# Layer A of two joined attentions: values issued behind the next group's scores

## The chip, the cores and the metric

The kernel runs on one core of a Trainium2 chip. The metric is device time in microseconds of one execution; the median of three runs stands for the kernel.

## The reference

Two attention layers over a sequence of 2048 rows with 1024 features, 32 heads of 32, in fp32; their outputs are joined along the last axis.

```python
# layer A: each query sees 8 keys, at distances 0, 2, ..., 14
idx = pos[:, None] - (jnp.arange(8) * 2)[None, :]
logits = einsum("bhsd,bhswd->bhsw", q, k[idx]) * scale      # masked where idx < 0
o = einsum("bhsw,bhswd->bhsd", softmax(logits), v[idx])
# layer B: each query sees the 256 keys up to itself
scores = einsum("bhqd,bhkd->bhqk", q, k) * scale            # masked outside the band
o = einsum("bhqk,bhkd->bhqd", softmax(scores), v)
# both: qkv = x @ wqkv before, o @ wo after
```

## The kernel before

**Units and groups.** The host lays the inputs out anew; layer A's rows are parted into even and odd ones, so that its dilated window becomes a plain band of 8. Each layer is four chunks of 512 rows. A chunk is a *unit* (layer B is units 0 to 3, layer A units 4 to 7), and in a unit the 32 heads are eight *groups* of four. `hg = 8 * u + s` numbers the groups, 0 to 63; layer A's are 32 to 63, and where the text counts "the 12th scores" it counts from 1 within layer A. In layer A half of the units have a `halo`: the last 8 keys and the last block of values of the unit before.

**Projections.** The large products, called g here (each into a tile `g` in PSUM), take most of TensorE's time: queries and keys (line 586), values into `vbuf` (line 654; 512 columns wide for groups 0 to 3, 256 wide for groups 4 and 5 and for 6 and 7), the output product of layer B (line 714), and the output product of layer A (line 773), which runs at the end. Each fp32 product is built of three products of parts (`TERMS`); ScalarE and VectorE cut the parts (lines 218, 221, 224) from tiles that POOL loads (line 173).

**Layer A's attention.** A group's queries and keys come out of `g` by ScalarE (lines 482 and 487) into `nat`; eight DMAs on the queue of SP gather them by head (line 506). `window` then builds two pieces of work for TensorE. `scores` (line 923) is 64 products of 32x32 tiles. VectorE adds the mask (line 931), takes the softmax (lines 941 to 959, with ScalarE's exponential on line 947) and transposes (line 961); ScalarE copies the result in eight pieces into a band of zeros called `wide` (lines 970 and 973). `values` (line 984) is 16 products, 20 with a halo, of `vbuf` by `wide`, each 32 columns of weights. `finish` copies them out of PSUM on ScalarE (line 1032), and SP stores them to `od` in DRAM (line 1037).

**What sets the order.** Nothing is scheduled by the compiler: while the program is built, a planner keeps a clock for each engine (`Clock`) and writes the instructions down in the order of its own simulation. Four sequences compete for TensorE: `aux`, `twos` (the values, in order), `ones` (the scores, in order) and `gemm` (the projections, in order). At each step the planner asks the head of each sequence when it could start, takes the earliest, and of equal ones the first in the order just given. What the piece triggers on other engines is issued at the planned times, so the order on ScalarE, VectorE and SP follows from the order on TensorE. For the values the question is `values_ready`: the group's part of `vbuf` is there, the last copy into `wide` is done, and the one PSUM bank for `o` is free. `done["scores"]` is filled by `seat_free` as soon as the scores of a group are issued.

The order that comes out, in pieces: in layer A TensorE has 55 unbroken runs of projections, with scores and values between them; of the 32 groups, 9 have their values right behind the scores of the next group, and 23 have them between projections.

## Time and profile before

| | us |
|---|---|
| median of three runs | 1814.6 (1813.79 to 1816.29) |
| profiled execution | 1818.1 |
| its span, first to last instruction | 1816.4 |
| TensorE busy with matmuls | 1789.4 (99%) |
| VectorE busy | 1262.0 (69%) |
| ScalarE busy | 924.4 (51%) |
| granted TensorE clock, mean | 0.995 |

The profile shows one execution. PE is TensorE's matmuls, PEld its weight loads, which run beside them; DVE is VectorE, ACT ScalarE, POOL GpSimd, SP the engine that only issues DMAs. A row of the timeline merges neighbouring instructions of one line: start, length, engine, line, operation, tile written and tiles read, count, and in brackets the idle time ahead of them with what ended it. "issue" is time in which the engine waited for nothing that the profile shows. The matmuls of the scores and values are in plain fp32 and count twice in the trace: 64 are x128. Since matmuls are pipelined, the ends overlap; distances are taken from start to start.

### The profile page before, as it was taken

The page shows a single profiled execution, that of the slowest core. Times are in us where ns is not written, and L with a number is a line of the kernel's source. Part 1 is how long each engine was busy: PE and PEld are TensorE (multiplying, and loading weights), DVE is VectorE, ACT ScalarE, POOL GpSimd, SP SyncE. Part 2 cuts the span into 40 slices and gives each one's busy share as a digit, 9 for nine tenths or more (in the row PEclk, how much of TensorE's full clock was granted, in tenths as well). Part 3 has the DMA queues.
Part 4 walks back from the last instruction along what each step waited for, and adds up shares of the span by engine and source line. Part 5 has one row for each costly group of instructions (what it writes and reads, how often), then busy time and mean ns, then how long its engine had stood idle before and what let it go on. Part 6 is the DMA issues. An engine that isn't in the chain of part 4 may idle for free.

```text
span 1816.4 us, 38617 instructions
## 1 busy us (share of the span) xinstructions
PE 1789.4 (99%) x14730; PEld 1465.3 (81%) x14730; DVE 1262.0 (69%) x2790; ACT 924.4 (51%) x2301; POOL 410.1 (23%) x950
## 2 busy tenths in 40 slices
PE   9999999999999999999999999999999999999999
PEld 6787878888777788778887788888888887888887
DVE  6677876768867769777677566646755766557866
ACT  5556466555655565656555344423542544446342
POOL 2313323222242223333224300101010011002220
PEclk9999999999999999999999999999999999999999
DMA  7354664544646555454545343536753674348984
GB/s 239 114 142 136 183 168 139 167 139 137 183 139 177 146 144 170 134 166 128 160 110 164 106 150 119 164 123 213 249 173 113 221 250 137 120 144 297 311 265 145
DMA packets 129241, 303.61 MB, mean 167 GB/s; under 512 B 16160, under 2 KB 31520, under 8 KB 129056
## 3 DMA queue, kind: packets, MB, share of 16 engines
q0 software_dynamic: 45216, 164.65, 28.7%
q1 hardware_dynamic: 73472, 116.56, 22.8%
q10 hardware_dynamic: 10368, 19.93, 3.0%
q8 instruction: 117, 1.92, 0.4%
q14 instruction: 68, 0.56, 0.1%
HBM read 189.79 MB, written 44.04 MB: 129 GB/s over the span
## 4 chain that ended last, share of the span: by engine, by line
PE 91%; DMA 3%; ACT 2%; DVE 2%; issue 1%; SPq 0%; POOL 0%; ACTq 0%; DVEq 0%; POOLq 0%
PE g L586 37%; PE g L654 18%; PE g L714 10%; PE g L773 8%; PE s L1172 5%; PE s L1089 5%; PE o L1219 5%; PE s L923 2%; PE o L984 2%; DMA r<-od 2%; DMA raw<-xs 1%; ACT wide L970 1%; ACT s L1099 0%; DVE w L224 0%; DVE r L846 0%
## 5 line engine op out<-in xcount | busy, mean ns | idle before, releaser
L586 PE MATMUL g<-x,w 128*128 128x512 f32 x3072 | 773.0, 396 | 2.8 <-ACT x L218 2.6
L586 PEld LDWEIGHTS g<-x,w 128*128 128x128 f32 x3072 | 568.1, 189 | 114.5 <-issue 6.8
L654 PE MATMUL g<-w,x 128*128 128x256 f32 (+1 forms) x2304 | 393.7, 322 | 0.5 <-issue 0.3
L224 DVE TENSOR_TENSOR w<-raw,w 128x512 fp32r<-128x512 f32 x518 | 339.4, 697 | 51.8 <-ACT w L218 45.1
L654 PEld LDWEIGHTS g<-w,x 128*128 128x128 f32 x2304 | 334.5, 192 | 28.8 <-issue 1.6
L1099 ACT ACTIVATE s<-s,nm 128x384 f32<-128x384 f32 (+2 forms) x512 | 274.4, 537 | 101.8 <-DVE nm L1094 101.6
L1094 DVE CUSTOM_DVE_ANT_0 s<-s,mask_d 128x384 f32<-128x384 f32 (+2 forms) x512 | 261.7, 554 | 88.1 <-PE s L1089 87.4
L1158 POOL TENSOR_SCALAR_AFFINE_SELECT pbuf<-pbuf 128x128 f32<-128x128 f32 (+1 forms) x606 | 220.1, 391 | 326.2 <-ACT pbuf L1179 324.8
L1179 ACT ACTIVATE pbuf<-s 128x384 f32<-128x384 f32 (+2 forms) x480 | 202.8, 505 | 73.7 <-PE s L1172 72.1
L714 PE MATMUL g<-r,w 128*128 128x512 f32 x768 | 190.8, 394 | 1.4 <-ACT r L1054 0.7
L173 POOL DMA_DIRECT2D raw<-wqk x126 | 68.6, 545 | 440.8 <-DVE w L224 303.0
L714 PEld LDWEIGHTS g<-r,w 128*128 128x128 f32 x768 | 141.9, 188 | 30.7 <-DVE r L1058 1.6
L773 PE MATMUL g<-x,w 128*128 128x512 f32 x672 | 153.2, 390 | 0.5 <-DVE w L224 0.5
L773 PEld LDWEIGHTS g<-x,w 128*128 128x128 f32 x672 | 126.0, 188 | 27.3 <-DVE w L224 0.9
L221 DVE CAST w<-raw 128x1024 fp32r<-128x1024 f32 x187 | 129.3, 692 | 25.2 <-PE g L586 22.6
L1172 PEld LDWEIGHTS s<-qst,kst 128*128 128x128 f32 x704 | 113.3, 189 | 40.6 <-ACT s L1099 16.2
L1089 PE MATMUL s<-kst,qst 96*128 96x384 f32 (+2 forms) x512 | 142.5, 342 | 0.9 <-ACT s L1099 0.7
L1172 PE MATMUL s<-qst,kst 128*128 128x256 f32 (+2 forms) x704 | 136.4, 302 | 3.5 <-ACT s L1099 3.0
L1089 PEld LDWEIGHTS s<-kst,qst 96*128 96x128 f32 x512 | 93.5, 189 | 25.8 <-issue 3.9
L931 DVE TENSOR_TENSOR band<-s,near 128x160 f32<-128x160 f32 x128 | 32.5, 316 | 116.0 <-PE s L923 116.0
L1099 ACT ACTIVATION_READ_ACCUMULATOR s<-s,nm 128x1 f32 x512 | 105.4, 206 | 0.0
L970 ACT COPY wide<-band 32x512 f32<-32x512 f32 x128 | 79.0, 618 | 49.2 <-DVE band L961 47.2
(81 smaller groups left out, 1405.7 us busy)
## 6 DMA issues: line engine op xcount, KB each, us to landing
raw<-wqk POOLq DMA_DIRECT2D x126, 512.0 KB, 4.3
raw<-wv POOLq DMA_DIRECT2D x72, 512.0 KB, 4.9
qst<-nat SPq DMA_DIRECT2D x96, 256.0 KB, 5.4
kst<-nat SPq DMA_DIRECT2D x96, 256.0 KB, 5.5
raw<-wo POOLq DMA_DIRECT2D x44, 512.0 KB, 4.4
raw<-xs POOLq DMA_DIRECT2D x28, 512.0 KB, 4.5
outs<-ost ACTq DMA_DIRECT2D x37, 256.0 KB, 2.8
kst<-halo SPq DMA_DIRECT2D x72, 128.0 KB, 4.4
```

Source lines behind the costliest of these rows:

```text
L221: nc.vector.tensor_copy(t[:, 0, :], raw)
L224: nc.vector.tensor_tensor(t[:, 1, c:c + 512], raw[:, c:c + 512], t[:, 0, c:c + 512].bitcast(F32), op=ALU.subtract)
L586: nc.tensor.matmul(h["ps"], h["w"][:, a, k * P:(k + 1) * P], xt[u][k][:, b, :], start=(k == 0 and i == 0), stop=(k == NK - 1 and i == 2))
L654: nc.tensor.matmul(ps, xt[u][kw * g + k][:, a, p0:p0 + P], h["w"][g][:, c, k], start=(first and t == 0 and half == 0), stop=(last and t == 2),
L714: nc.tensor.matmul(h["ps"], w[:, a, c:c + P], ot[u, k][:, b, :], start=(k == 0 and i == 0), stop=(k == NK - 1 and i == 2))
L773: nc.tensor.matmul(h["ps"], w[:, a, c:c + P], x[:, b, :], start=(k == 0 and t == 0), stop=(k == 3 and t == 2))
L1089: nc.tensor.matmul(ps[:, :n], q[0:96, j, b * P:(b + 1) * P], kk[0:96, j, c0:c1], start=True, stop=True)
L1094: nc.vector.tensor_tensor_reduce(ps[:, :n], ps[:, :n], mask[:, cut:full], scale=-1.0, scalar=BIG, op0=ALU.add, op1=ALU.min, accum_out=nm)
L1099: nc.scalar.activation(ps[:, :n], ps[:, :n], AF.Exp, bias=nm, scale=-1.0, accum_out=sm)
L1158: nc.gpsimd.affine_select(w, w, pattern=[[0, m], [step, n]], compare_op=ALU.is_ge, fill=0.0, base=base, channel_multiplier=chan)
L1172: nc.tensor.matmul(ps[:, i * n:(i + 1) * n], kk[:, j, 256 + kb * P:256 + (kb + 1) * P], q[:, j, q0:q0 + n], start=True, stop=True)
L1179: nc.scalar.activation(w, ps[:, :pack * n].rearrange("p (j n) -> p j n", j=pack), AF.Exp)
```

## The change

Values of a group in layer A are now held back until the scores of the next group have been issued; with `hg + 3 < 64` the last three groups are left out of the rule. Since values stand ahead of scores and projections in the planner's choice, they come next behind those scores, unless something else is missing (their part of `vbuf`, for example).

```diff
         def values_ready():
+            if hg + 3 < U * NG and hg + 1 not in done["scores"]:
+                return None
             return latest(done["v"].get((u, vp)), h.get("p"), ro.when())
```

In the program that is built, 21 groups of layer A have their values right behind scores, and there are 43 runs of projections. Lines of the kernel behind 976 move down by two (the values are line 986 afterwards).

## The prediction

> **What bounds the kernel now.** First the page: its totals, the instruction queue, the chain that ended last.

> ```profile
> span 1816.4 us, 38617 instructions
> PE 1789.4 (99%) x14730; PEld 1465.3 (81%) x14730; DVE 1262.0 (69%) x2790; ACT 924.4 (51%) x2301; POOL 410.1 (23%) x950
> q8 instruction: 117, 1.92, 0.4%
> PE 91%; DMA 3%; ACT 2%; DVE 2%; issue 1%; SPq 0%; POOL 0%; ACTq 0%; DVEq 0%; POOLq 0%
> ```

> TensorE is the bound: 99% busy and 91% of the chain. A change of order can gain only what PE loses between its instructions. Next, the waits of PE in the stretch that the change touches, 1040 to 1660 us (layer A's 32 groups):

> ```profile
> PE o L984 <- ACT wide L973: 3.8, 3, 2.5
> PE s L923 <- issue: 1.9, 2, 1.4
> PE o L984 <- issue: 2.6, 1, 2.6
> PE o L984 <- DVE vbuf L610: 0.9, 1, 0.9
> PE g L773 <- DVE w L224: 0.5, 1, 0.5
> PE g L654 <- issue: 0.3, 1, 0.3
> ```

> Columns: total us, how often, longest. It is 10.0 us in all: 3.8 for the copies that build `wide`, 4.8 under "issue", that is, for nothing that another engine does, and 1.4 at the end of the stretch, where the order stays as it is. The projections (g) wait for no weights, so data feeds PE in time.

> What a switch costs isn't a wait here; it hides in the spacing of starts. From PE's timeline (start, length; s = scores, 64 matmuls shown as 128; o = values; g = projections):

> ```profile
> 1066.14 1.32 PE L923 MATMUL s<-pbuf 32*32 32x40 f32 x128
> 1067.39 1.12 PE L984 MATMUL o<-wide,vbuf 128*32 128x136 f32 x32
> 1068.44 11.86 PE L586 MATMUL g<-x,w 128*128 128x512 f32 x51
> 1080.23 1.12 PE L984 MATMUL o<-wide,vbuf 128*32 128x136 f32 x32
> 1081.28 8.45 PE L586 MATMUL g<-x,w 128*128 128x512 f32 x36
> 1089.66 1.32 PE L923 MATMUL s<-pbuf 32*32 32x40 f32 x128
> ...
> 1377.92 19.33 PE L586 MATMUL g<-x,w 128*128 128x512 f32 x84
> 1397.18 1.32 PE L923 MATMUL s<-pbuf 32*32 32x40 f32 x128
> ```

> By starts, 84 projections take 19.26 us, 51 take 11.79 and 36 take 8.38: (19.26 - 8.38)/48 = 0.2267 each, and 8.38 - 36 x 0.2267 = 0.22 for each unbroken run, whatever its length. Values take 1.05 us (1080.23 to 1081.28), and behind scores also 1.05 (1067.39 to 1068.44). So values between projections break a run in two and pay 0.22 once more; behind scores they don't. The weight loads show the same gap:

> ```profile
> 1067.39 0.85 PEld L984 LDWEIGHTS o<-wide,vbuf 128*32 128x32 f32 x32
> 1080.23 0.85 PEld L984 LDWEIGHTS o<-wide,vbuf 128*32 128x32 f32 x32 [0.35 <-issue]
> ```

> 0.35 us ahead of values that follow projections (scores there have it too), none between scores and values. [...]

> **The change, part by part.** Counted in the order of the built programs: of 32 groups, 9 have their values right behind scores before, 21 after; the runs of projections in layer A fall from 55 to 43. No instruction is added or removed, except that PE has 446 semaphore waits for 440. Layer B's order is the same, and so is everything from the scores of group 27 on.

> *1. Twelve runs fewer.* Nine of the vanished breaks end in 512-column projections at 0.22; three in 256-column ones, priced from these rows:

> ```profile
> 1286.47 8.89 PE L654 MATMUL g<-w,x 128*128 128x256 f32 x72
> 1295.29 1.32 PE L923 MATMUL s<-pbuf 32*32 32x40 f32 x128
> ...
> 1441.94 10.34 PE L654 MATMUL g<-w,x 128*128 128x256 f32 x84
> 1452.21 1.32 PE L923 MATMUL s<-pbuf 32*32 32x40 f32 x128
> ```

> 72 take 8.82, 84 take 10.27: 0.121 each and 0.12 a run. 9 x 0.22 + 3 x 0.12 = **-2.3 us**. Ends: -1.4 (all at 0.12) and -4.2 (all at the 0.35 of the weight load).

> *2. The waits for `wide`, 3.8 us in three places.* A 0.18 us wait (unit 4's group 7) goes, since its values now wait for later scores. One of 1.09 us (unit 5's group 6) keeps its place, with 3 more projections ahead, and PE gets there about 0.9 later: 0.2 stays. The third (unit 6's group 6), on PE:

> ```profile
> 1500.88 1.50 PE L984 MATMUL o<-wide,vbuf 128*32 128x136 f32 x32 [2.54 <-ACT wide L973]
> ```

> and on ScalarE's timeline there:

> ```profile
> 1497.01 0.62 ACT L970 COPY wide<-band 32x512 f32<-32x512 f32 x1 [3.04 <-DVE band L961]
> ...
> 1500.85 0.60 ACT L482 ACTIVATE nat<-g 128x512 f32<-128x512 f32 x1
> ```

> The planner now puts 30 projections, not 24, before these values, but on ScalarE it moves the evacuation of the 24th (L482) ahead of the eight copies. They then start only after PE's 24th projection plus 0.1 + 0.6, and last 3.85 (1497.01 to 1500.85); PE covers 6 x 0.227 + 0.1. The wait is about 3.05. Together 3.8 becomes 3.25: **-0.6 us**. Ends: -3.8 (all gone), +3 (a second place like it). What else waits on the values is off the path: their evacuation (0.59 on ScalarE), the store of `od` on SP, now behind up to two further gathers of `nat`, and the next use of `wide` are due a group later, and no projection waits for a cast today.

> *3. PE's instruction stream.* This part speaks against the change. The rows behind "issue":

> ```profile
> 1117.92 2.20 PE L654 MATMUL g<-w,x 128*128 128x256 f32 x17 [0.35 <-issue]
> ...
> 1157.92 0.26 PE L923 MATMUL s<-pbuf 32*32 32x40 f32 x4 [1.41 <-issue]
> ...
> 1490.92 0.33 PE L923 MATMUL s<-pbuf 32*32 32x40 f32 x23 [0.53 <-issue]
> ...
> 1594.89 1.32 PE L923 MATMUL s<-pbuf 32*32 32x40 f32 x128
> 1596.14 0.95 PE L984 MATMUL o<-wide,vbuf 128*32 128x8 f32 x29
> 1599.64 0.64 PE L984 MATMUL o<-wide,vbuf 128*32 128x136 f32 x11 [2.55 <-issue]
> ```

> And the DMA view of 1597.1 to 1598.2 us, in the middle of the last wait:

> ```profile
> q8 instruction: 1, 0.02, 5.1%
> ```

> One packet of the instruction queue lands there, and PE goes on about 1.5 us later. Queue 8 is PE's: 14730 weight loads, 14730 matmuls and 443 further entries of its sequencer are 29903, over 117 packets 256 each. Numbered in that order, the four waits stand at instructions 15042, 16065, 24258 and 26818: 256k + 450 with k = 57, 61, 93, 103. So packet k is needed at 256k + 450. None of the last 69 packets starts before 256k + 157; allowing a microsecond for the request, I estimate that it is asked for at 256k + 144, 306 ahead. In projections that is 35 us; but scores issue 256 instructions in 1.25 us, and values 64 to 80 more in 1.05. Scores alone are shorter than 306; **scores with values, 320 to 336, are longer**, so a packet can be asked for and missed inside one burst. From asking to going on, the last wait took 4.7 us (1594.95 to 1599.64), the first 4.6; the other two 6.0 and 7.1. One packet (k = 84) had 3.8 us and came in time. I take 4.2 for a new place, between 3.8 and 4.6.

> With the new order, worked out from the same spacings, five packets get less than that: k = 68 has 3.46 us (waits 0.75), 70 3.32 (0.9), 76 4.0 (0.2), 80 2.05 (2.15), 98 3.02 (1.2). The places: right after the values behind the 11th scores, in those behind the 12th, after those behind the 15th, in those behind the 17th, right after those behind the 26th. The four old waits keep theirs. Sum **+5.2 us**. Ends: 3.4 (all at 3.8) and, lower still, 0 if requests come earlier than I estimate; 9.7 at 5.1, the mean of layer A's 63 packets from asking to landing, plus 1.4.

> *Sum.* -2.3 - 0.6 + 5.2 = **+2.3 us**. The profiled execution took 1818.1 us (span 1816.4), 3.5 above the median 1814.6 of the runs; I add to the median: **1816.9**.

> **The rivals.**
> *A. The instructions come in time.* If the new packets are early, only parts 1 and 2 are left: 1814.6 - 2.9 = **1811.7**. For it: 0.4% of DMA time on q8, and by that last reckoning a sixth of layer A's packets took under 3.8 us. Against it: 2.55 us lost in one of just nine pairs. [...]
> *B. The packets come late* (slower). At 5.1 us each the five places cost 9.7: 1814.6 - 2.9 + 9.7 = **1821.4**. It decides from about 4.5 us a packet. For it: two of four old waits had 6.0 and 7.1, while activations were being loaded.
> *C. ScalarE.* Every moved evacuation delays a cast of weights by its 0.59 us: 12 x 0.59 = 7, so 1823.9. Against it: the projections of layer A wait for no cast, and ScalarE is 51% busy.
> *D. The change doesn't do what it says.* Only 12 of 32 groups move; 11 still stand alone. If gaps and fetches cancel, 1814.6.

> **How the numbers follow.** A measurement can tell about 0.2%, 3.6 us, from no change: faster is below 1811.0, slower above 1818.2. Forecast 0.50, spread 1814.5 to 1819.5 (0.38 same, 0.12 slower); A 0.17 (0.07 faster, 0.10 same); B 0.22 and C 0.05, slower; D 0.06, same. Faster 0.07, same 0.54, slower 0.39. The range 1811.0 to 1823.0 leaves out 0.07 below and some 0.09 above.

> **What would show it.** Part 1: 43 runs, no 0.35 us gap ahead of the values that moved. Part 2: one wait of about 3 us for `wide` before the values of unit 6's group 6. Part 3: "issue" waits of PE near 10 us instead of 4.8, at the five places, each ending some 1.5 us behind a packet of q8. "Issue" still near 5 means A; 13 and more, B; a projection waiting for ACT or DVE, C.

## The result, and the profile after

The changed kernel takes **1820.0 us** (median of 22 runs, 1814.35 to 1824.36); the kernel before, run beside it, 1815.9 (22 runs, 1810.87 to 1820.46). The ratio is **1.0024, 95% interval [1.0015, 1.0034]**: slower, by little more than the 0.2% that can be told from no change (the interval reaches down to 0.15%). The profiled execution took 1821.89 us, its span is 3.7 us longer than before.

First the waits of PE in the same stretch as in the prediction, 1040 us to the end of layer A's values (1664 us now); columns as there: total us, how often, longest.

```profile
PE o L986 <- issue: 4.7, 3, 2.8
PE g L586 <- DVE w L221: 2.6, 1, 2.6
PE s L923 <- issue: 1.7, 1, 1.7
PE o L986 <- DVE vbuf L610: 1.4, 1, 1.4
PE o L986 <- ACT wide L973: 1.0, 1, 1.0
PE g L714 <- issue: 0.6, 1, 0.6
PE g L773 <- DVE w L224: 0.5, 1, 0.5
PE g L586 <- issue: 0.5, 1, 0.5
```

"issue" went from 4.8 to 7.5 us; the projections, which before waited for weights only at the end of the stretch (0.5 us, line 773, in both), wait once more, 2.6 us, for VectorE's cast of weights (line 221). On PE's timeline of the changed kernel, one run of projections that was broken before, and then the places of the instruction packets:

```profile
1068.79 20.70 PE L586 MATMUL g<-x,w 128*128 128x512 f32 x90
1089.41 1.32 PE L923 MATMUL s<-pbuf 32*32 32x40 f32 x128
1090.66 1.12 PE L986 MATMUL o<-wide,vbuf 128*32 128x136 f32 x32
...
1157.92 0.26 PE L923 MATMUL s<-pbuf 32*32 32x40 f32 x5 [1.73 <-issue]
...
1248.19 0.62 PE L714 MATMUL g<-r,w 128*128 128x512 f32 x2 [0.60 <-issue]
...
1275.37 0.89 PE L986 MATMUL o<-wide,vbuf 128*32 128x136 f32 x24 [0.36 <-issue]
...
1367.25 0.87 PE L986 MATMUL o<-wide,vbuf 128*32 128x136 f32 x19 [1.49 <-issue]
...
1560.45 10.61 PE L586 MATMUL g<-x,w 128*128 128x512 f32 x46 [0.46 <-issue]
...
1602.98 1.10 PE L986 MATMUL o<-wide,vbuf 128*32 128x136 f32 x14 [2.85 <-issue]
```

90 projections take 20.62 us from start to start, which is 90 x 0.2267 + 0.22: one fixed part instead of two. The six waits that follow are packets 61, 68, 70, 80, 98 and 103, each at instruction 256k + 449 or 450. Of the five new places that the forecast named, four are here; packet 76 was in time.

One thing that no step of the forecast held shows in the table by stretches, one microsecond a row (columns: stretch, busy time of PE, PEld, DVE, ACT and POOL with the number of instructions, then PEclk, DMA share, GB/s). Before, behind the wait for packet 61 (1.41 us):

```profile
1158.00:1159.00 1.00, 1.00 (x11) 0.95 (x12) 1.00 (x2) 0.18 (x1) 0.00 (x0) 1.00 0.86 328
1159.00:1160.00 1.00, 1.00 (x10) 1.00 (x9) 1.00 (x3) 1.00 (x3) 0.00 (x0) 1.00 0.14 41
1160.00:1161.00 1.00, 1.00 (x8) 0.91 (x7) 1.00 (x3) 0.88 (x2) 0.46 (x1) 1.00 0.00 0
```

And after, behind the same wait, now 1.73 us:

```profile
1158.00:1159.00 1.00, 1.00 (x12) 0.95 (x13) 0.96 (x2) 0.22 (x1) 0.00 (x0) 0.96 0.86 172
1159.00:1160.00 1.00, 1.00 (x7) 1.00 (x7) 1.00 (x2) 0.92 (x2) 0.00 (x0) 0.50 0.80 315
1160.00:1161.00 1.00, 1.00 (x6) 1.00 (x6) 1.00 (x3) 0.56 (x1) 0.00 (x0) 0.50 0.16 57
1161.00:1162.00 1.00, 1.00 (x6) 0.90 (x5) 1.00 (x3) 0.31 (x2) 0.72 (x1) 0.50 0.00 0
```

PEclk is 0.50: for 3.41 us TensorE runs at half its clock, six or seven matmuls in a row of the table instead of eight to eleven, and loses about 1.5 us. The kernel before has two such spells in layer A (at 1501 and 1600 us, behind its two longest waits); the changed one has three.

**Where the time went**, span against span, by the starts of PE's instructions in the two traces:

| | forecast | traces |
|---|---|---|
| twelve runs of projections fewer | -2.3 | -2.6 |
| waits for `wide` and weights, units 4 to 6 | -0.6 | +0.3 |
| five new packet places | +5.2 | +3.9 |
| four old packet places | 0 | -0.4 |
| half-clock spell behind packet 61 | not seen | +1.5 |
| wait for `vbuf` at the end (0.9, now 1.4) | 0 | +0.5 |
| the rest, each under 0.5 (0.3 of it ahead of layer A) | 0 | +0.5 |
| sum | +2.3 | +3.7 |

Without the spell the traces add up to +2.2, beside the forecast's +2.3. That agreement is partly luck: the terms that came out lower than forecast (by 0.3, 1.3 and 0.4) and those that came out higher (by 0.9, 0.5 and 0.5) nearly cancel.

One profile is one execution. Over all runs the mean granted clock points the same way: 0.99678 in the 23 runs of the kernel before that stood beside e1 to e4 (0.99664 and 0.99665 beside the later experiments), 0.99550 in the 22 of the changed one. The difference, 0.0011 to 0.0013 of 1818 us, is 2.1 to 2.3 us, with a standard error of some 0.9 from the spread of the single runs. So of the 4.1 us between the medians about half is lost clock, and what is left, about 2 us, is near the 2.3 that the forecast made without any.

### The profile page after: what moved, and what is told of

It is laid out like the page before. It is cut to its first block, busy times and chain, and to the rows that moved or that the text cites. A ratio compares the mean times of both kernels' runs of the same rounds, so it can differ in the third digit from the quotient of the medians.

```text
span 1820.1 us, 38632 instructions
## 1 busy us (share of the span) xinstructions
PE 1790.5 (98%) x14730; PEld 1465.8 (81%) x14730; DVE 1262.3 (69%) x2791; ACT 925.6 (51%) x2300; POOL 410.1 (23%) x950
## 3 DMA queue, kind: packets, MB, share of 16 engines
q8 instruction: 117, 1.92, 0.4%
## 4 chain that ended last, share of the span: by engine, by line
PE 91%; DMA 3%; DVE 3%; ACT 2%; issue 1%; SPq 0%; POOL 0%; ACTq 0%; DVEq 0%; POOLq 0%
PE g L586 37%; PE g L654 18%; PE g L714 9%; PE g L773 8%; PE s L1174 5%; PE s L1091 5%; PE o L1221 5%; PE s L923 2%; PE o L986 2%; DMA raw<-xs 1%; DMA r<-od 1%; DVE w L224 1%; ACT s L1101 0%; DVE x L224 0%; DMA outs<-ost 0%
## 5 line engine op out<-in xcount | busy, mean ns | idle before, releaser
L586 PE MATMUL g<-x,w 128*128 128x512 f32 x3072 | 770.8, 395 | 5.8 <-DVE w L221 2.6
L586 PEld LDWEIGHTS g<-x,w 128*128 128x128 f32 x3072 | 568.5, 189 | 117.6 <-issue 10.1
L654 PE MATMUL g<-w,x 128*128 128x256 f32 (+1 forms) x2304 | 393.7, 322 | 0.4 <-DVE w L224 0.2
L224 DVE TENSOR_TENSOR w<-raw,w 128x512 fp32r<-128x512 f32 x518 | 339.5, 697 | 64.2 <-ACT w L218 57.5
L654 PEld LDWEIGHTS g<-w,x 128*128 128x128 f32 x2304 | 334.7, 192 | 29.4 <-issue 1.7
L773 PE MATMUL g<-x,w 128*128 128x512 f32 x672 | 153.2, 390 | 0.5 <-DVE w L224 0.5
L773 PEld LDWEIGHTS g<-x,w 128*128 128x128 f32 x672 | 125.9, 188 | 27.3 <-DVE w L224 0.9
L970 ACT COPY wide<-band 32x512 f32<-32x512 f32 x128 | 79.1, 618 | 48.3 <-DVE band L961 46.3
```

The costliest lines, as they stand in the source:

```text
L224: nc.vector.tensor_tensor(t[:, 1, c:c + 512], raw[:, c:c + 512], t[:, 0, c:c + 512].bitcast(F32), op=ALU.subtract)
L586: nc.tensor.matmul(h["ps"], h["w"][:, a, k * P:(k + 1) * P], xt[u][k][:, b, :], start=(k == 0 and i == 0), stop=(k == NK - 1 and i == 2))
L654: nc.tensor.matmul(ps, xt[u][kw * g + k][:, a, p0:p0 + P], h["w"][g][:, c, k], start=(first and t == 0 and half == 0), stop=(last and t == 2),
L773: nc.tensor.matmul(h["ps"], w[:, a, c:c + P], x[:, b, :], start=(k == 0 and t == 0), stop=(k == 3 and t == 2))
```

## The experiments

The theory: instruction packets that come late make the loss, at places set by the order and by where the borders of 256 instructions fall. The rival: the new order makes PE wait for other engines (ScalarE, VectorE, loads), and "issue" is a by-product. Two tools serve all kernels. *Tiny products* are 32x32 products behind the warm-up, each four PE instructions, overwritten by what follows: they compute nothing and only shift the borders. `since[0]` counts the steps of projections since the last scores (a step is three products of 512 columns or six of 256), and a *hold* makes values wait for eight such steps, 24 projections or more, so that they stand alone. Runs of projections are counted here from layer A's first scores to its last values, 54 before and 42 after; the prediction counts the one behind them too.

```diff
+    since = [0]
...
+        since[0] = 0 if name == "1" else since[0] + (name == "g")
```

**e1: the kernel before, borders shifted by 188 instructions.**

```diff
         for i in range(WARM):
             nc.tensor.matmul(ps, idle[:, :P], idle, start=True, stop=True)
+        few = idle.bitcast(F32)
+        for i in range(47):
+            nc.tensor.matmul(ps[0:32, 0:32], few[0:32, 0:32], few[0:32, 0:32], start=True, stop=True)
```

> The kernel before with 188 more instructions of TensorE at the start (47 tiny products, about half a microsecond, in a stretch where TensorE waits for the first loads); order and work of everything behind are unchanged, only the borders of the 256-instruction packets move. Fetch theory (a packet that is asked for 306 instructions ahead and comes 4.2 us later): the places where a packet is missed change from k = 103 to three others of 2.1 to 2.3 us each behind scores with values, the sum of the waits for instructions rises from about 2.5 to 7.1 by that reckoning, so 4 to 5 us slower than before, 1820, with 'issue' waits of 8 to 10 us. Rival (the loss of the changed kernel comes from the order of the work on ScalarE and VectorE): nothing changes, 1815.9, 'issue' as before.

1821.4 us (7 runs) beside 1815.5: 1.0032 [1.0021, 1.0043], without any change to the order. On its timeline the old places are empty, and PE waits at 256k + 449 or 450 with k = 56, 90 and 102:

```profile
1106.58 0.42 PE L984 MATMUL o<-wide,vbuf 128*32 128x128 f32 x7 [2.39 <-issue]
...
1455.00 1.11 PE L984 MATMUL o<-wide,vbuf 128*32 128x136 f32 x29 [0.83 <-issue]
...
1584.92 0.89 PE L984 MATMUL o<-wide,vbuf 128*32 128x136 f32 x14 [2.74 <-issue]
```

With the order unchanged, PE's stops have moved with the count of instructions. The time is about the theory's 1820, but "issue" is only 5.9 us, for 8 to 10 expected and 4.8 before. Beside it the trace has three half-clock spells in layer A for two, later waits for the gathers (1.6) and for `vbuf` (2.0 for 0.9), and shorter ones for `wide` (2.8 for 3.8).

**e2: every group held, none behind scores.** `if hg + 3 < U * NG and since[0] < 8: return None` in `values_ready`.

> The opposite of the change: in layer A values wait until eight steps of projections have been issued behind the last scores, so that none but one stands right behind scores (62 runs of projections instead of 55). Fetch theory: the seven more runs cost 1.6 us, the 2.55 us wait in the values behind the 29th scores goes and with it the slow clock behind it (1.5 us); 1813 to 1814, 'issue' waits about 2 us. Rival (what counts is the gap at each run, instructions come in time or late by chance): 1.6 us slower than before, 1817.5.

A miss: 1826.0 (5 runs), 1.0053 [1.0039, 1.0067]. The waits of PE in 1040 to 1680 us:

```profile
PE s L924 <- issue: 4.4, 2, 2.2
PE o L987 <- ACT wide L974: 3.3, 3, 2.6
PE g L587 <- DVE w L224: 2.8, 2, 1.5
PE g L587 <- DVE w L221: 1.9, 1, 1.9
PE g L587 <- ACT w L218: 1.6, 1, 1.6
```

The theory failed here in two ways. Two packets (61 and 89) were missed inside scores alone, 6.9 and 7.1 us after the estimated request, where 4.2 had been allowed. And the rival is partly right: 9.6 us are waits for ScalarE and VectorE, 5.2 before, since the holds change the order on those engines too. Four half-clock spells follow for two before, one of them twice as long, and there are 62 runs of projections, 1.8 us more.

**e3: the change without four of its five packet places.** The rule gets `and hg not in (41, 42, 47, 56)`; these groups keep the planner's own place. 46 runs of projections.

> The change with four more groups left out of its rule: those whose values would stand behind the 11th, 12th, 17th and 26th scores, where packets 68, 70, 80 and 98 were missed. 46 runs instead of 43. Fetch theory: the four new waits go, 1.9 us of gaps stay saved; 1814 (1.9 below before, 6 below the change). Rival (order on ScalarE and VectorE): eight or nine of twelve moves remain, so some 3 us of the loss, 1819.

1815.9 (11 runs), 1.0008 [0.9999, 1.0017]: four groups carried most of the loss. The time lies between the theory's 1814 and the rival's 1819, nearer to the first. Three new places are gone, and packet 68 keeps 0.19 us; on PE's timeline what "issue" is left stands at old places:

```profile
1116.20 2.29 PE L654 MATMUL g<-w,x 128*128 128x256 f32 x17 [0.52 <-issue]
...
1156.09 0.27 PE L923 MATMUL s<-pbuf 32*32 32x40 f32 x5 [1.47 <-issue]
...
1596.88 0.65 PE L986 MATMUL o<-wide,vbuf 128*32 128x136 f32 x15 [2.40 <-issue]
```

**e4: the change with holds at seven places.** The rule is `since[0] < 8` for groups 41, 42, 45, 47, 49, 56 and 59 and that of the change for the others; 51 runs.

> Both rules together: values wait for the next scores, except in the seven groups where a packet of instructions would be missed in the burst (the four, and those behind the 15th, 19th and 29th scores); there they wait for eight steps of projections behind the last scores. 51 runs. Fetch theory: 0.9 us of gaps saved, the new waits gone, the old 2.55 us one and the slow clock behind it gone too; 1811 to 1812, faster than both kernels. Rival (order on ScalarE and VectorE): between the two kernels, 1816 to 1820.

A miss by 4 us: 1815.8 (11 runs), 1.0001 [0.9987, 1.0015]. By 4.2 us a packet 0.1 us of waits should have been left. There were 4.5, in places that had been taken for safe: packet 68 took about 8 us from the estimated request and packet 109 7.5. A wait of 2.1 us for ScalarE in unit 6 stayed, with a spell behind it. The profiled execution took 1812.1 us, 3.7 less than the median, so its trace doesn't show all that the other runs lost.

**e5 and e6: the changed kernel, borders shifted** by 204 and by 52 instructions (51 and 13 tiny products, as in e1).

> The changed kernel with 51 tiny products (204 PE instructions, overwritten by what follows) behind the warm-up; the order is untouched, only the borders of the instruction packets move against it. Fetch theory: at 4.2 us a packet the waits inside layer A fall from 8.0 to 5.8 us, all in other places (packet 56 in values, 71 right behind values, 85, 102 in values, 110 in values; none at the old places in the values behind the 17th and the 29th scores), and none is much over 1.7 us, so the half-clock spells behind such waits go too: 1816 to 1818 us. Rival (the loss is in waits for other engines that the new order brings): as the changed kernel, 1820.

> The changed kernel with 13 tiny products (52 PE instructions) behind the warm-up: the borders move to where they hurt most. Fetch theory: waits of 10.5 us in all at 4.2 us a packet (packets 66: 2.2, 68: 1.4, 74: 1.4, 76: 2.4, 86: 1.8, 98: 1.0), two or three of them long enough for a half-clock spell: 1822.5 to 1825 us. Rival: as the changed kernel, 1820.

e6 goes the way of the theory, and 3 us further than its range: 1828.2 (6 runs) beside 1815.95, 1.0064 [1.0049, 1.0079], with "issue" at 13.3 us in layer A for 10.5 expected. Five of the six packets named for it wait (98 was in time) and four others (72, 80, 92 and 105); two waits, of 2.4 and 3.7 us, have spells behind them. e5 is a miss: 1822.7 (9 runs), 1.0046 [1.0031, 1.0061], no better than the changed kernel. Three of the five places named for it wait (56, 71 and 110), and four others that had been taken for safe (64, 90, 94 and 104), 10.2 us of "issue" in all for 5.8 expected. From its timeline:

```profile
1104.27 0.66 PE L986 MATMUL o<-wide,vbuf 128*32 128x136 f32 x15 [0.29 <-issue]
...
1278.32 9.54 PE L586 MATMUL g<-x,w 128*128 128x512 f32 x34 [4.71 <-issue]
```

Packet 71 was asked for at about 1270.5, by the prediction's estimate of the request, and needed 7.9 us. The stretch from that request to the packet's start, in the table by stretches:

```profile
1270.50:1275.60 5.10, 3.11 (x170) 2.39 (x168) 2.66 (x6) 0.59 (x1) 0.00 (x0) 1.00 0.91 286
```

The DMA engines were 91% busy. For packet 80 of the changed kernel (4.2 us in all) they were 40% busy from the estimated request to the start:

```profile
1363.00:1364.80 1.80, 1.78 (x120) 1.31 (x120) 0.00 (x0) 1.17 (x2) 0.00 (x0) 1.00 0.40 141
```

That made a new question: does a packet wait behind bulk traffic?

**e9: the kernel before with more DMA traffic.**

```diff
+    spare = [dram.tile([P, 1024], F32, name=f"spare{i}") for i in range(4)]
...
         def scores():
+            for i in range(2):
+                nc.scalar.dma_start(spare[2 * (hg % 2) + i], wqk[0, i])
             qk = rows[hg]
```

> The kernel before, with two further copies of 512 KB from DRAM to DRAM at the scores of each of layer A's 32 groups, which nobody reads. It leaves nothing out. Counted from instruction 256k + 144, layer A's 63 instruction packets start on the DMA engines 2.57 us later on the average in the kernel before. Theory (a packet waits in the DMA engines behind bulk traffic; in the runs so far the mean is 1.9 us with the engines under 10% busy and 3.2 over 85%): the mean rises to 3.0 or more, and the waits of PE under issue in layer A from 4.8 us to 7 or more. Rival (the time of a packet has nothing to do with the traffic, the spread is chance): 2.6 us and 4 to 6 us of waits. The time itself may rise for waits for weights as well and tells little.

A hit. The table by stretches, 1040 to 1660 us in one row:

```profile
1040.00:1660.00 620.00, 602.25 (x7602) 502.21 (x7601) 372.72 (x631) 255.97 (x483) 60.99 (x109) 0.99 0.66 215
```

The DMA share is 0.66 (0.53 before), and layer A's packets start 3.62 us after the estimated request instead of 2.57 (62 and 63 packets; in the other eleven profiles the mean is 2.5 to 2.9); 27 of them take over 4 us, 14 before. PE's timeline has packet 103 in the same values as before, where 2.55 us were waited:

```profile
1613.44 1.09 PE L987 MATMUL o<-wide,vbuf 128*32 128x136 f32 x11 [4.76 <-issue]
```

"issue" is 10.2 us for 4.8. The one run took 1837.5 us; 6.3 of that are waits for the gathers, of which the profile before shows none.

**e7: the kernel before with a single hold,** for the 28th group, whose values met packet 103. `if hg == 59 and since[0] < 8: return None`.

> The kernel before, in which one group only (the 28th of layer A) no longer has its values right behind the next scores: they wait for 24 projections more. Two runs of projections more, +0.4 us. Fetch theory: the wait of 2.55 us for packet 103 in those values goes, and with it the half-clock spell behind it (about 1.5 us): 1812 us. Rival (the packet is late anyway, or the next wait takes its place): 1815.5 to 1816.

A hit: **1811.9** (11 runs) beside 1815.95, 0.9984 [0.9972, 0.9995]. On its timeline the scores and the values of that group are apart, and nothing waits:

```profile
1591.29 1.32 PE L924 MATMUL s<-pbuf 32*32 32x40 f32 x128
1592.54 1.66 PE L587 MATMUL g<-x,w 128*128 128x512 f32 x6
1594.03 4.47 PE L655 MATMUL g<-w,x 128*128 128x256 f32 x36
1598.43 1.18 PE L987 MATMUL o<-wide,vbuf 128*32 128x8 f32 x40
1599.55 4.57 PE L655 MATMUL g<-w,x 128*128 128x256 f32 x36
```

This is the reverse of the change at one place: splitting one pair pays, because the pair (336 instructions) is longer than the estimated lead of a packet (306). This profile has no half-clock spell in layer A, though packet 93 waits 2.2 us in it, for 0.5 before.

**e8: the same, shifted by 16 instructions.**

> The same with 4 tiny products (16 PE instructions) behind the warm-up, which move the borders of packets 57, 61 and 84 off the bursts and bring one hazard of 0.5 us (packet 72). Fetch theory: the old waits of 0.35, 1.4 and 0.5 us go or move, 1811 to 1812 us. Rival: as the kernel before, 1815.5.

A miss: 1814.1 (12 runs), 0.9986 [0.9977, 0.9996], no further gain. Packets 57, 61 and 84 are off the bursts, but packets 68, 72 and 86 wait in their place (1.9, 0.8 and 0.8 us).

**e10: the change with holds at the five groups that met packets,** 41, 42, 47, 56 and 59; 48 runs.

> The change without its packet hazards: its rule, except for five groups (the 10th, 11th, 16th, 25th and 28th), whose values wait for 24 projections behind the scores instead. 48 runs of projections for 55, 8 fewer than the kernel before with the 28th group held. If instruction packets and what hangs on them were all of the loss: 8 x 0.22 = 1.8 us under that kernel, 1810 us. If the new order also costs on the data side (unit 6's waits for ScalarE and VectorE, the wait at the end): 1813 to 1816.

1812.7 (11 runs), 0.9984 [0.9975, 0.9994], at the edge of the second case. Five groups held turn the change from 1.0024 to 0.9984; but one of the five is e7's group 59, and that hold alone gives the kernel before the same 0.9984. So without its packet places the change costs nothing that the times show, and its eight runs fewer than e7 bought nothing that they show either: in unit 6 a projection still waits, with a spell behind it. The two longest of PE's waits in 1040 to 1680 us:

```profile
PE g L587 <- DVE w L221: 2.9, 1, 2.9
PE s L924 <- issue: 2.5, 2, 1.7
```

**e11: the hold of e7, and the change's rule in units 4 and 5 alone,** where no packet is near (not for groups 41, 42, 45 and 47); 52 runs.

> The kernel before with the 28th group held as above, and the rule of the change in the first two units of layer A alone, without the four groups that meet a packet there: 52 runs of projections, 4 fewer than with the hold alone, all in places without a packet and away from units 6 and 7. Part 1 of the prediction: 0.9 us under the kernel with the hold alone, 1811 us; the runs can hardly tell that, the trace can: the sum of projection runs' fixed parts falls by 4 x 0.22 and nothing new waits. Rival (a break costs nothing by itself, the order only moves idle time): 1812 us, and the 0.9 us come back as waits.

**1810.9** (12 runs), 0.9979 [0.9970, 0.9988]: the lowest median of all these kernels, faster than both the kernel before and the changed one. Its 1.0 us under e7 fits the 0.9 expected, but the intervals overlap; that part is not shown. Nor does the trace settle it: it was expected that nothing new waits, and in its trace packet 109 waits 2.7 us with a spell behind it, and the values of unit 6 wait 3.1 us for `wide`, 0.6 in e7's.

## Why the prediction was right and wrong

The forecast was 1816.9 with "within 0.2%" as likeliest (0.54) and "slower" at 0.39. The time, 1820.0, lies in the range, the sign is right, and so is the mechanism that the sign came from, the packets. Of the 3.1 us that were missing, 1.3 lie in the kernel before itself (its median is 1814.6 over the three runs that the forecast started from, 1815.9 over 22) and 1.8 in the change; together they were enough to pass from "the same" to "slower".

*Part 1, twelve runs fewer: right.* 43 runs, and the sum of the fixed parts falls by 12 x 0.22 = 2.6, not 2.3: the three breaks that the forecast priced at 0.12 also end in 512-column projections (line 654 for groups 0 to 3). From the start of scores to that of the values behind them it is 1.25 us (1089.41 to 1090.66 above), as before.

*Part 2, the waits for `wide`: the order was right, the place and the size were not.* On ScalarE the evacuation of the 24th projection (line 482) does stand ahead of the copies:

```profile
1501.32 0.60 ACT L482 ACTIVATE nat<-g 128x512 f32<-128x512 f32 x1 [3.63 <-PE g L586]
1501.82 0.60 ACT L970 COPY wide<-band 32x512 f32<-32x512 f32 x1
...
1505.24 0.29 ACT L973 COPY wide<-band 32x128 f32<-32x128 f32 x1
```

and on PE's timeline the wait came six projections earlier than said, for weights:

```profile
1495.66 5.63 PE L586 MATMUL g<-x,w 128*128 128x512 f32 x24
1503.91 2.90 PE L586 MATMUL g<-x,w 128*128 128x512 f32 x6 [2.62 <-DVE w L221]
1506.74 1.25 PE L986 MATMUL o<-wide,vbuf 128*32 128x136 f32 x32
```

VectorE's row says why: its cast of these weights starts at 1503.08, behind the softmax steps of two groups.

```profile
1502.33 0.82 DVE L943 TENSOR_TENSOR band<-band,nm 128x640 f32<-128x640 f32 x1
1503.08 0.69 DVE L221 CAST w<-raw 128x1024 fp32r<-128x1024 f32 x1
```

The sentence that no projection waits for a cast was true of the trace of before, but for the 0.5 us of line 773 at the end, and was carried over to an order in which six more projections come ahead of the values. With the spell that follows in both kernels the place costs as much as before (about 4.2 us by starts). In unit 5 the wait that was to fall from 1.09 to 0.2 us is 0.98, since the copies into `wide` came later too. So the gain of 0.6 is gone; rival C saw the kind, not the size.

*Part 3, the packets: right in place, a quarter too large.* Four of the five named places wait, by starts 0.8, 0.6, 1.9 and 0.6 us; packet 76 (0.2 forecast) does not. No trace shows a request: the place 256k + 144, the microsecond allowed in it and the lead of 306 are the author's estimate. The four took 3.5 to 4.2 us from the estimated request, in and below the lower half of the 3.8 to 4.6 that had been taken. (Packet 84 of the kernel before, from which the 3.8 came, had 4.3 by its trace.) e3 and e10 show that these places made most of the loss. (Rival A had the instructions in time; e1 and e7, which change little but where a packet's border meets a burst, decide against that: 1.0032 and 0.9984.) Two of the four old waits didn't keep theirs: packet 93 was in time, and packet 57 cost 0.3 us by starts instead of 0.5.

*What failed was the unspoken step that a wait costs its own length.* The wait for packet 61 grew by only 0.3 us, and the half-clock spell behind it cost 1.5; no term of the sum held it. Rival B (packets late, 1821.4) came nearer to the time, though not to the change (+6.8, the forecast +2.3, measured +4.1), and for the wrong reason: the new packets were early, not late.

*What the forecast's one figure for a packet hid.* 4.2 us served the changed kernel: at three of its new places (packets 68, 80 and 98) the DMA engines were 3, 40 and 6% busy from the estimated request to the packet's start. At the fourth, packet 70, they were full, and it took about 4 us all the same. The figure did not serve e2, e4 and e5, where eight packets took 6 to 9 us, with the engines 80% busy or more. e9 shows the load to be a cause of the mean (2.57 to 3.62 us, with a DMA share of 0.53 to 0.66); it doesn't foretell the single packet.

What makes one wait of about 2 us bring a spell and the next none, no run isolates. In these profiles it goes with the place of the wait among steps of 3.4133 us, which lie differently to the kernel's start from profile to profile (last section). So the spell behind packet 61 is taken to belong to this execution; of the others only the mean clock is on record. Left open: how the 0.5 us at the end (`vbuf`) hangs on the earlier places, and whether the 0.22 us of a saved break comes back in the time.

## What to carry to other kernels

Before short instructions are packed together, count them: where a burst issues more instructions than the estimated lead with which the next packet is asked for (306 here), the saved switch can be paid back as a wait, and by the prices of this case one such place (2.6 us and a spell of 1.5 for packet 103) outweighs ten saved switches. A shorter burst isn't safe under load: e2 missed two packets inside scores alone, with the DMA engines 80 and 92% busy. A wait of TensorE may cost more than its length: the 1.73 us for packet 61 had a half-clock spell behind them that lost 1.5 us more. A change is worth taking apart by place: the rule as a whole lost 0.24%; with five groups held it was 0.16% ahead, and a single hold on the kernel before (e7), without the rule, was as much ahead.

## What the hardware did that was not expected

The spread of the runs goes with the clock: over the 22 runs of the changed kernel time and mean clock have a correlation of -0.73, and the fastest run (1814.35) had a mean clock of 0.999, the three slowest (1823.9 to 1824.4) 0.993 and 0.994.

**Instruction packets start later under load.** In the same profiles a packet of layer A starts 1.9 us after the estimated request on the mean where the DMA engines are under 10% busy in the 1.2 us behind it (some 180 packets) and 3.3 us where they are over 85% busy (some 290); the slowest started 10 us after it. In the ten waits for packets that the kernels before and after have in layer A, PE goes on 1.2 to 1.6 us after the packet has landed.
